# Spreading 1/den over each head's partitions: copies on the SP queue in place of 0/1 matrix products, in a one-core attention and gMLP kernel

## The chip, the cores and the metric

The kernel runs on one core of a Trainium2 chip. Its engines work side by side and meet through semaphores: TensorE (PE) multiplies matrices out of SBUF into PSUM, VectorE (DVE), ScalarE (ACT) and GpSimd (POOL) work on elements, SyncE (SP) issues DMA transfers. The metric is device time in microseconds (us) of one launch, lower is better.

## The reference

B = 1, S = 2048, D = 512, H = 32 heads of Dh = 16, F = 1792; inputs in bfloat16. The first block is linear attention, the second a gMLP that mixes along the sequence.

```python
def _A_ref(x, wqkv, wo):
    qkv = (x @ wqkv).reshape(B, S, 3, H, Dh).transpose(2, 0, 3, 1, 4)
    q, k, v = qkv[0], qkv[1], qkv[2]
    phi = lambda t: jnp.where(t > 0, t + 1, jnp.exp(t)) + 1e-06
    pq, pk = phi(q), phi(k)
    kv = jnp.einsum('bhsd,bhse->bhde', pk, v)
    z = jnp.einsum('bhsd->bhd', pk)
    num = jnp.einsum('bhqd,bhde->bhqe', pq, kv)
    den = jnp.einsum('bhqd,bhd->bhq', pq, z)[..., None] + 1e-06
    o = num / den
    return o.transpose(0, 2, 1, 3).reshape(B, S, D) @ wo

def _B_ref(x, w_in, w_sp, b_sp, w_out):
    z = gelu_tanh(x @ w_in)
    z1 = z[..., :Fh]
    z2 = _layernorm(z[..., Fh:])
    g = jnp.einsum('ts,bsf->btf', w_sp, z2) + b_sp[None, :, None]
    return (z1 * g) @ w_out

x = A_x
h = x + _A_ref(_layernorm(x), A_wqkv, A_wo)
h2 = h + _B_ref(_layernorm(h), B_w_in, B_w_sp, B_b_sp, B_w_out)
```

## The kernel before

The sequence is cut into 16 tiles of 128 rows; four tiles make a group of 512 (gq or tg, 0 to 3). The feature dimension of 512 lies in four chunks (c, 0 to 3) of 128 partitions, each with 8 heads of 16.

Stage by stage: tiles of x are loaded, normalised on DVE (L568 statistics, L572 aggregate, L603) and transposed into xT, tiles 0 to 5 on PE (L633), tiles 6 to 15 by DMA transposes on SP's queue (L625). PE makes K (L715) and Q (L729); phi is Exp and Relu on ACT (L692, L694) and one or two operations on DVE (L695, then L698 or L701). V is never made: PE sums x'K over all tiles (L747), and once that is complete makes K'V from it (L796). DVE masks K'V to its heads' diagonal blocks (L806), PE multiplies it by Wo (L814), and ACT and DVE copy the two halves out (L819, L821). With that, a group's attention output is phi(Q) times this matrix (L879), which DVE adds to x (L884).

Before L879, phi(Q) is divided by den. `den(gq)` multiplies phi(Q) by the summed keys (L829, four products into 32 partitions each, one row of 512 for each head), and ACT makes 1/den as Ln and Exp (L834, L836), in bfloat16 in `rb_v`. PE spreads each head's row over the head's 16 partitions with a 0/1 matrix `sel` (L844, four products with 32 rows, into PSUM). For chunks 0 and 1 ACT copies the result to SBUF (L854) and DVE multiplies from there (L856); for chunks 2 and 3 DVE multiplies straight out of PSUM (L859). POOL builds `sel` at the start (L542, L545).

The second block: h is normalised on ACT (L610), transposed by DMA on SP's queue into hT (L625), multiplied by w_in (L911 for z2, L942 for z1), with Gelu on ACT (L916, L947) and the layer norm of z2 on DVE. PE mixes z2 with w_sp' (L981); w_sp comes in through 64 DMA transposes on SP's queue (L957). The last product is w_out (L999), to which DVE adds h (L1005) and SP stores the tile (L1007); the last tile goes in two halves of 256 columns.

POOL issues the loads of Wv, w_in and Wo (L492), which wait for the landing of the last xT transpose; the first wsp transpose stands behind the same transpose on SP's queue.

Nothing decides at run time. Each `op` names its engine and what it reads and writes; `ORDER` is a list of all operations by number, written out by hand, from which each engine's own order follows, and `SLOT` gives the PSUM banks and buffers. Every engine works strictly in its order, and a wait stops whatever stands behind it on that engine. A DMA's issue is an operation of the engine that issues it. The numbers `cost` and `land` in an `op` don't change what runs.

Of the kernel before, what the change touches and what calls it, by code (L numbers as in the profile page):

```python
# [6 lines left out]
BF16 = mybir.dt.bfloat16  # L7
ACT = mybir.ActivationFunctionType
# [43 lines left out]
]  # L52
SLOT = [
# [301 lines left out]
def bass_sequential_preLN__linear_attn_block__mixer_gmlp__prompt_kernel(  # L355
# [29 lines left out]
    COPY_DVE = ()  # L385
    LN1 = [[0], [1], [2], [3], [4, 5], [6, 7], [8, 9], [10, 11], [12, 13], [14, 15]]
    N2_ACT = range(16)
    VIA_ACT = ((0, 0), (1, 0), (2, 0), (3, 0))
# [32 lines left out]
    gz2 = View(s_kv, 0, [NT, FH], BF16)  # L421
    mw = View(s_kv, NT * FH * 2, [KD, D], BF16)
# [16 lines left out]
    sel = small([P], BF16)  # L439
# [32 lines left out]
    def bank(i):  # L472
        return lambda a: a[:, i, :]
# [68 lines left out]
    op("pool", 0.2, lambda e: e.memset(sel.all().ap(), 0.0), w=[sel.all()], bias=BIG)  # L542
    sel3 = sel.ap.rearrange("p (b e) -> p b e", e=DH)
    for c in range(KD):
        op("pool", 0.35, lambda e, c=c: e.affine_select(  # L545
            sel3, sel3, pattern=[[-(CG * DH // P), P // DH], [0, DH]], compare_op=ALU.not_equal, fill=1.0,
            base=-CG * c, channel_multiplier=1), r=[sel.all()], w=[sel.all()], bias=BIG)

# [274 lines left out]
    def den(gq):  # L823
        t = Tile(PS)
        r_ = pqT[gq].all()

        def mm(e):
            for c in range(KD):
                i = e.matmul(t(bank(0)).ap()[CG * c:CG * (c + 1), :], lhsT=zb.ap[:, CG * c:CG * (c + 1)],  # L829
                             rhs=r_.ap()[:, c, :], start=True, stop=True)  # L830
            return i
        op("pe", 0.23, mm, r=[zb.all(), r_], w=[t()], land=3.0)
        rr, rb = rr_v[gq, :], rb_v[gq, :]
        op("act", act_c(512, 1), lambda e: e.activation(rr.ap(), t(bank(0)).ap(), ACT.Ln, bias=eps[1:2].ap(),  # L834
                                                        scale=1.0), r=[t(), eps[1:2]], w=[rr])
        o = op("act", act_c(512), lambda e: e.activation(rb.ap(), rr.ap(), ACT.Exp, scale=-1.0), r=[rr],  # L836
               w=[rb])
        last_lnexp.append(o)
        spread = {0: Tile(PS, 2), 2: Tile(PS, 2)}

        def sp_(e):
            for c in range(KD):
                q0 = CG * c
                k = e.matmul(spread[c // 2 * 2](bank(c % 2)).ap(), lhsT=sel.ap[q0:q0 + CG, :],  # L844
                             rhs=rb.ap()[q0:q0 + CG, :], start=True, stop=True)
            return k
        op("pe", 0.23, sp_, r=[sel.all(), rb], w=[spread[0](), spread[2]()], land=4.0)
        for c0 in (0, 2):
            t2 = spread[c0]
            d = pqT[gq][c0:c0 + 2, :]  # L850
            if (gq, c0) in VIA_ACT:
                e_ = Tile(EB)
                b_ = e_(lambda a: a[:, 0:2 * GW])
# [8 lines left out]
    for gq in range(NG):  # L862
        g.bias = -QGROUP * gq
        if gq:
            for f in (0, 2):
                q_proj(gq, f)
        den(gq)
# [210 lines left out]
```

## Time and profile before

| what | value |
|---|---|
| median of 3 runs | 244.15 us (244.04 to 244.27) |
| profiled execution's own time | 243.96 us |
| span of the profiled execution, first to last instruction | 242.2 us |
| granted TensorE clock | 1.00 |
| L844 on PE | 16 matmuls, 384 ns mean |
| L854 on ACT | 4, 1034 ns mean |
| L859 on DVE, out of PSUM | 4, 1204 ns mean |
| L856 on DVE, out of SBUF | 4, 681 ns mean |
| last two stores (64 KB each) | 1.5 us from issue to landing |

The span starts at the first instruction of the profiled execution; what is left of its own time, 1.8 us, lies before and after. Matmuls are pipelined, so the mean of one (379 ns for 512 columns) is longer than the distance between two starts; the timeline, which gives starts, tells how fast PE moves on. SP's time is time of issuing, not of the transfer.

### The profile page before, as it was taken

Reading aid. Unit: us, or ns where it says so; the run is one execution under the profiler, and the core shown is the slowest. Engines: PE = TensorE matmul, PEld = TensorE weight load, DVE = VectorE, ACT = ScalarE, POOL = GpSimd, SP = SyncE. Lnnn points to the kernel's source line nnn. Section 1 sums busy time; section 2 is a strip of 40 time slices with the busy share of each in tenths; the row PEclk is TensorE's granted clock in tenths of the full one; section 3 lists DMA queues with packets and bytes.
Section 4 is the critical chain, followed back from the end, with each engine's and each line's share of the span. In section 5 each row is a group of like instructions: output and inputs, shape, how many; then the busy total and the mean of one; then the engine's idle time right before and its main releaser. Section 6 shows DMA issues by size and latency. Waiting matters only on the chain.

```text
span 242.2 us, 3026 instructions
## 1 busy us (share of the span) xinstructions
PE 238.3 (98%) x1175; PEld 108.8 (45%) x1175; DVE 135.2 (56%) x269; ACT 85.1 (35%) x107; POOL 34.1 (14%) x87
## 2 busy tenths in 40 slices
PE   8999999999999999999999999999999999999995
PEld 3544443433444444445444444444444444444443
DVE  4999654589999967656533223251332513322443
ACT  3875744898588598564500010000000000000000
POOL 5316021002316542122100000000000000000000
DMA  6920459954324231459344444446200100000022
GB/s 199 321 43 18 94 106 337 232 122 96 46 43 128 47 46 22 87 119 231 88 108 92 107 86 95 100 108 94 83 0 0 65 24 0 0 0 3 0 87 87
DMA packets 55598, 21.57 MB, mean 89 GB/s; under 512 B 49472, under 2 KB 54720, under 8 KB 55584
## 3 DMA queue, kind: packets, MB, share of 16 engines
q1 hardware_dynamic: 54640, 17.05, 32.7%
q0 software_dynamic: 944, 4.33, 5.5%
q8 instruction: 9, 0.15, 0.3%
q14 instruction: 5, 0.04, 0.1%
HBM read 7.47 MB, written 2.10 MB: 40 GB/s over the span
## 4 chain that ended last, share of the span: by engine, by line
PE 91%; DVE 4%; DMA 2%; ACT 2%; SPq 1%; issue 0%
PE ps L981 40%; PE ps L942 10%; PE ps L911 10%; PE ps L999 10%; PE ps L747 6%; PE ps L879 5%; PE ps L715 5%; PE ps L729 4%; DMA xh<-in_A_x_dram 2%; DVE small L568 1%; SPq L492 1%; DVE xT_pq_z L698 1%; DVE xh L884 0%; DVE xT_pq_z L859 0%; DVE e L695 0%; PE ps L844 0%
## 5 line engine op out<-in xcount | busy, mean ns | idle before, releaser
L981 PE MATMUL ps<-wsp,pk_xn_z 128*128 128x512 bf16 x336 | 73.8, 379 | 0.0
L988 DVE TENSOR_TENSOR e<-ps,e 128x512 bf16<-128x512 f32 x28 | 19.4, 691 | 66.0 <-PE ps L981 66.0
L981 PEld LDWEIGHTS ps<-wsp,pk_xn_z 128*128 128x128 bf16 x336 | 32.8, 98 | 39.5
L942 PE MATMUL ps<-hT,win 128*128 128x512 bf16 x112 | 26.6, 379 | 0.0
L911 PE MATMUL ps<-win,hT 128*128 128x512 bf16 (+1 forms) x128 | 26.0, 353 | 0.0
L999 PE MATMUL ps<-wout,xT_pq_z 128*128 128x512 bf16 (+1 forms) x119 | 24.7, 367 | 0.0
L981 PE MATMUL ps<-wqkv_wsp,pk_xn_z 128*128 128x512 bf16 x112 | 24.3, 379 | 0.0
L947 ACT ACTIVATE xT_pq_z<-ps 128x1024 bf16<-128x1024 f32 (+1 forms) x16 | 14.4, 913 | 23.9 <-PE ps L942 23.9
L568 DVE BATCH_NORM_STATS2 small<-xh 128x6 f32<-128x512 bf16 x32 | 20.7, 678 | 3.3 <-DMA xh<-in_A_x_dram 3.3
L920 DVE BATCH_NORM_STATS2 small<-pk_xn_z 128x6 f32<-128x512 bf16 (+1 forms) x32 | 18.3, 611 | 7.2 <-ACT pk_xn_z L916 7.1
L692 ACT ACTIVATE e<-ps 128x1024 bf16<-128x1024 f32 x16 | 16.5, 1029 | 9.7 <-PE ps L715 6.1
L911 PEld LDWEIGHTS ps<-win,hT 128*128 128x128 bf16 x128 | 12.5, 98 | 12.7 <-ACT e L854 0.3
L916 ACT ACTIVATE pk_xn_z<-ps 128x896 bf16<-128x896 f32 x16 | 14.5, 914 | 8.9 <-PE ps L911 8.8
L1005 DVE TENSOR_TENSOR e<-ps,xh 128x512 bf16<-128x512 f32 (+1 forms) x17 | 11.2, 660 | 11.3 <-PE ps L999 11.3
L999 PEld LDWEIGHTS ps<-wout,xT_pq_z 128*128 128x128 bf16 x119 | 11.6, 98 | 12.8
L981 PEld LDWEIGHTS ps<-wqkv_wsp,pk_xn_z 128*128 128x128 bf16 x112 | 11.0, 98 | 13.2
L942 PEld LDWEIGHTS ps<-hT,win 128*128 128x128 bf16 x112 | 10.9, 98 | 12.6 <-ACT pk_xn_z L916 0.4
L589 POOL TENSOR_TENSOR small<-small 128x2 f32<-128x2 f32 x22 | 16.0, 727 | 1.2
L587 POOL TENSOR_SCALAR small<-small 128x2 f32<-128x2 f32 x22 | 6.4, 297 | 67.6 <-DVE small L572 67.4
L747 PE MATMUL ps<-pk_xn_z 128*128 128x512 bf16 x64 | 15.6, 379 | 0.0
L729 PE MATMUL ps<-xT_pq_z,wqkv_wsp 128*128 128x512 bf16 x64 | 15.5, 380 | 0.0
L715 PE MATMUL ps<-wqkv_wsp,xT_pq_z 128*128 128x512 bf16 x64 | 15.3, 379 | 0.0
(72 smaller groups left out, 191.0 us busy)
## 6 DMA issues: line engine op xcount, KB each, us to landing
out_dram<-e SPq DMA_DIRECT2D x15, 128.0 KB, 1.7
win<-in_B_w_in_dram POOLq DMA_DIRECT2D x1, 1792.0 KB, 9.2
xh<-in_A_x_dram SPq DMA_DIRECT2D x5, 256.0 KB, 4.7
wqkv_wsp<-in_A_wqkv_dram SPq DMA_DIRECT2D x2, 512.0 KB, 5.7
wout<-in_B_w_out_dram POOLq DMA_DIRECT2D x1, 896.0 KB, 6.4
wsp<-in_B_w_sp_dram SPq DMA_TRANSPOSE x48, 2.9
xh<-in_A_x_dram SPq DMA_DIRECT2D x1, 512.0 KB, 6.2
wqkv_wsp<-in_A_wqkv_dram POOLq DMA_DIRECT2D x1, 512.0 KB, 4.8
```

What stands on the lines that cost most here:

```text
L568: op("dve", dve_c(512), lambda e: e.bn_stats(s6.ap(), src.ap()), r=[src], w=[s6])
L589: return op("pool", 0.7, lambda e: e.tensor_tensor(dst.ap(), dst.ap(), h.ap(), ALU.pow), r=[dst, h], w=[dst])
L692: op("act", act_c(n), lambda e: e.activation(lo.ap(), t(flat).ap(), ACT.Exp), r=[t()], w=[lo])
L715: i = e.matmul(t(bank(ti)).ap(), lhsT=lhs.ap()[:, c, :], rhs=rhs.ap()[:, c, :], start=(c == 0), stop=(c == KD - 1))
L729: r_ = e.matmul(t(bank(i)).ap(), lhsT=lhs.ap()[:, c, :], rhs=rhs.ap()[:, c, :], start=(c == 0), stop=(c == KD - 1))
L747: r = e.matmul(txk[h](bank(i)).ap(), lhsT=xx.ap()[:, c * P:(c + 1) * P], rhs=kk.ap(), start=(n == 0), stop=(n == NT - 1))
L911: k = e.matmul(t(bank(i)).ap()[:, 0:b - a], lhsT=l.ap()[:, c, :], rhs=win[c, a:b].ap(), start=(c == 0), stop=(c == KD - 1))
L920: op("dve", dve_c(b - a), lambda e, s6=s6, src=src: e.bn_stats(s6.ap(), src.ap()), r=[src], w=[s6])
L942: k = e.matmul(t(bank(i)).ap(), lhsT=l.ap()[:, c, :], rhs=r_.ap()[:, c, :], start=(c == 0), stop=(c == KD - 1))
L981: k = e.matmul(t(bank(0)).ap(), lhsT=l.ap()[:, s - a, :], rhs=r_.ap()[:, s - a, :], start=(s == 0), stop=(s == NT - 1))
L988: op("dve", dve_c(512), lambda e: e.tensor_tensor(gb().ap(), t(bank(0)).ap(), bsp().ap()[:, tg * GW:(tg + 1) * GW], ALU.add), r=[t(), bsp( ...
L999: k = e.matmul(t(bank(0)).ap()[:, 0:b - a], lhsT=l.ap()[:, fc, :], rhs=wout[fc, a:b].ap(), start=(fc == 0), stop=(fc == KF - 1))
```

## The change

1/den no longer goes through PE. Each group and chunk gets one SBUF-to-SBUF DMA copy on SP's queue: its source is 8 rows of `rb` (every fourth partition of the chunk's 32, since a head's row stands in four equal copies), each read 16 times, its destination a buffer `r_v` of 128 partitions x 512. The buffers lie where phi(K) and the normalised x were (tiles 12 to 15 of phi(K) for group 0, the normalised x for groups 1 to 3), so a copy also waits for the L747 products that read these. Chunks 0 and 1, and chunks 2 and 3, share a semaphore each; DVE multiplies two chunks at a time, from SBUF. `sel`, its five POOL instructions, the ACT copies and the PSUM tiles for the spread are gone. The last tile's output is stored as 384 and 128 columns.

`ORDER` and `SLOT` are new throughout. Line numbers move: L844, L854 and L859 are gone, the product is L843, the copy L839, den L823, the mask of K'V L796 (was L806), the product with Wo L807 (was L814), its copy out L814 (was L821), the attention product L867 (was L879).

```diff
-    VIA_ACT = ((0, 0), (1, 0), (2, 0), (3, 0))
+    DEN = [(0,), (1,), (2,), (3,)]
...
+    r_v = [View(s_kv, (3 + i) * KD * GW * 2, [KD, GW], BF16) for i in range(NG)]
...
-    sel = small([P], BF16)
...
-    op("pool", 0.2, lambda e: e.memset(sel.all().ap(), 0.0), w=[sel.all()], bias=BIG)
-    sel3 = sel.ap.rearrange("p (b e) -> p b e", e=DH)
-    for c in range(KD):
-        op("pool", 0.35, lambda e, c=c: e.affine_select(
-            sel3, sel3, pattern=[[-(CG * DH // P), P // DH], [0, DH]], compare_op=ALU.not_equal, fill=1.0,
-            base=-CG * c, channel_multiplier=1), r=[sel.all()], w=[sel.all()], bias=BIG)
...
-        spread = {0: Tile(PS, 2), 2: Tile(PS, 2)}
-
-        def sp_(e):
-            for c in range(KD):
-                q0 = CG * c
-                k = e.matmul(spread[c // 2 * 2](bank(c % 2)).ap(), lhsT=sel.ap[q0:q0 + CG, :],
-                             rhs=rb.ap()[q0:q0 + CG, :], start=True, stop=True)
-            return k
-        op("pe", 0.23, sp_, r=[sel.all(), rb], w=[spread[0](), spread[2]()], land=4.0)
+
+    def spread_mul(gq):
+        rb = rb_v[gq, :]
+        for c in range(KD):
+            r = r_v[gq][c, :]
+            src = rb.ap()[CG * c:CG * (c + 1):CG * DH // P, :].unsqueeze(1).to_broadcast([P // DH, DH, GW])
+            op("sp", 0.5, lambda e, r=r, src=src: e.dma_start(r.ap(), src), r=[rb], w=[r],
+               dma=(f"r{gq}{c // 2}", True), nbytes=P * GW * 2)
         for c0 in (0, 2):
-            t2 = spread[c0]
-            d = pqT[gq][c0:c0 + 2, :]
-            if (gq, c0) in VIA_ACT:
...
-            op("dve", dve_c(1024), lambda e, t2=t2, d=d: e.tensor_tensor(flat(d.ap()), flat(d.ap()), t2(flat).ap(),
-                                                                         ALU.mult), r=[d, t2()], w=[d])
+            d, m = pqT[gq][c0:c0 + 2, :], r_v[gq][c0:c0 + 2, :]
+            op("dve", dve_c(1024, 2), lambda e, m=m, d=d: e.tensor_tensor(flat(d.ap()), flat(d.ap()), flat(m.ap()),
+                                                                          ALU.mult), r=[d, m], w=[d])
...
-        project(n, [(0, D)] if n < NT - 1 else [(0, D // 2), (D // 2, D)])
+        project(n, [(0, D)] if n < NT - 1 else [(0, D - P), (D - P, D)])
```

More of the change, by code (lines that the diff above doesn't have):

```diff
@@ L821, in bass_sequential_preLN__linear_attn_block__mixer_gmlp__prompt_kernel, with den @@
             op("dve", dve_c(1024), lambda e, t=t, d=d: e.tensor_copy(d.ap(), t().ap()), r=[t()], w=[d])
-    def den(gq):
-        t = Tile(PS)
-        r_ = pqT[gq].all()
+    def den(gs):
+        t = Tile(PS, len(gs))
+        r_ = [pqT[gq].all() for gq in gs]
         def mm(e):
-            for c in range(KD):
-                i = e.matmul(t(bank(0)).ap()[CG * c:CG * (c + 1), :], lhsT=zb.ap[:, CG * c:CG * (c + 1)],
-                             rhs=r_.ap()[:, c, :], start=True, stop=True)
-            return i
[L832 to L836, printed above, removed]
+            for j in range(len(gs)):
+                for c in range(KD):
+                    i = e.matmul(t(bank(j)).ap()[CG * c:CG * (c + 1), :], lhsT=zb.ap[:, CG * c:CG * (c + 1)],
+                                 rhs=r_[j].ap()[:, c, :], start=True, stop=True)
+            return i
+        op("pe", 0.23 * len(gs), mm, r=[zb.all()] + r_, w=[t()], land=3.0)
+        rr, rb = rr_v[gs[0]:gs[-1] + 1, :], rb_v[gs[0]:gs[-1] + 1, :]
+        op("act", act_c(512 * len(gs), 1), lambda e: e.activation(rr.ap(), t().ap(), ACT.Ln, bias=eps[1:2].ap(),
+                                                                  scale=1.0), r=[t(), eps[1:2]], w=[rr])
+        o = op("act", act_c(512 * len(gs)), lambda e: e.activation(rb.ap(), rr.ap(), ACT.Exp, scale=-1.0), r=[rr],
@@ L837, in den @@
                w=[rb])
         last_lnexp.append(o)
-        spread = {0: Tile(PS, 2), 2: Tile(PS, 2)}
-        def sp_(e):
-            for c in range(KD):
-                q0 = CG * c
-                k = e.matmul(spread[c // 2 * 2](bank(c % 2)).ap(), lhsT=sel.ap[q0:q0 + CG, :],
-                             rhs=rb.ap()[q0:q0 + CG, :], start=True, stop=True)
-            return k
-        op("pe", 0.23, sp_, r=[sel.all(), rb], w=[spread[0](), spread[2]()], land=4.0)
-        for c0 in (0, 2):
-            t2 = spread[c0]
-            d = pqT[gq][c0:c0 + 2, :]
-            if (gq, c0) in VIA_ACT:
-                e_ = Tile(EB)
-                b_ = e_(lambda a: a[:, 0:2 * GW])
-                op("act", act_c(1024), lambda e, t2=t2, b_=b_: e.activation(b_.ap(), t2(flat).ap(), ACT.Copy),
-                   r=[t2()], w=[b_])
-                op("dve", dve_c(1024, 2), lambda e, b_=b_, d=d: e.tensor_tensor(flat(d.ap()), flat(d.ap()), b_.ap(),
-                                                                               ALU.mult), r=[d, b_], w=[d])
-                continue
-            op("dve", dve_c(1024), lambda e, t2=t2, d=d: e.tensor_tensor(flat(d.ap()), flat(d.ap()), t2(flat).ap(),
-                                                                         ALU.mult), r=[d, t2()], w=[d])
@@ new lines, in spread_mul @@
+    def spread_mul(gq):
+        rb = rb_v[gq, :]
+        for c in range(KD):
+            r = r_v[gq][c, :]
+            src = rb.ap()[CG * c:CG * (c + 1):CG * DH // P, :].unsqueeze(1).to_broadcast([P // DH, DH, GW])
+            op("sp", 0.5, lambda e, r=r, src=src: e.dma_start(r.ap(), src), r=[rb], w=[r],
+               dma=(f"r{gq}{c // 2}", True), nbytes=P * GW * 2)
+        for c0 in (0, 2):
+            d, m = pqT[gq][c0:c0 + 2, :], r_v[gq][c0:c0 + 2, :]
+            op("dve", dve_c(1024, 2), lambda e, m=m, d=d: e.tensor_tensor(flat(d.ap()), flat(d.ap()), flat(m.ap()),
+                                                                          ALU.mult), r=[d, m], w=[d])
@@ L866, in bass_sequential_preLN__linear_attn_block__mixer_gmlp__prompt_kernel @@
                 q_proj(gq, f)
-        den(gq)
+        for gs in DEN:
+            if gs[-1] == gq:
+                den(gs)
+                for j in gs:
+                    spread_mul(j)
     for gq in range(NG):
```

84 rows, old and new, of tables (ORDER, SLOT) are left out of this document.

## The prediction

> **What bounds the kernel now.** I read the page first: the busy shares and the chain that ended last.
>
> ```profile
> PE 238.3 (98%) x1175; PEld 108.8 (45%) x1175; DVE 135.2 (56%) x269; ACT 85.1 (35%) x107; POOL 34.1 (14%) x87
> ...
> PE 91%; DVE 4%; DMA 2%; ACT 2%; SPq 1%; issue 0%
> ```
>
> TensorE (PE) is the bound: 98% busy, 91% of the chain. Next, the waits of PE, which name hardly one:
>
> ```profile
> PE ps L633 <- DVE pk_xn_z L603: 0.4, 1, 0.4
> ```
>
> So a matmul that goes shortens the run by its own time, and an idle microsecond of PE lengthens it by one. Third, PE's timeline where the change sits (start, length of the merged row, line):
>
> ```profile
> 44.37 0.61 PE L829 MATMUL ps<-xT_pq_z,small 128*32 128x512 bf16 x8
> 44.91 1.04 PE L729 MATMUL ps<-xT_pq_z,wqkv_wsp 128*128 128x512 bf16 x4
> 45.79 1.06 PE L796 MATMUL ps<-wsp,wqkv_wsp 128*128 128x128 bf16 x16
> 46.78 0.40 PE L844 MATMUL ps<-wsp,small 32*128 32x512 bf16 x4
> 47.10 1.04 PE L729 MATMUL ps<-xT_pq_z,wqkv_wsp 128*128 128x512 bf16 x4
> 47.98 1.03 PE L814 MATMUL ps<-wqkv_wsp,wsp 128*128 128x512 bf16 x4
> ```
>
> Read the starts: 4 full matmuls move PE on by 0.86 (0.216 each), L796's 16 by 1.0, four spreads (L844) by 0.32. Last, the queue that the new copies must share, SP's own timeline (issues; the length is SP's time):
>
> ```profile
> 14.38 18.60 SPq L625 DMA_TRANSPOSE xT_pq_z<-pk_xn_z  x10
> 33.02 25.87 SPq L957 DMA_TRANSPOSE wsp<-in_B_w_sp_dram  x16
> 38.45 4.66 SPq L957 DMA_TRANSPOSE wsp<-in_B_w_sp_dram  x1
> 51.11 2.56 SPq L957 DMA_TRANSPOSE wsp<-in_B_w_sp_dram  x2
> 103.44 26.72 SPq L957 DMA_TRANSPOSE wsp<-in_B_w_sp_dram  x20
> ```
>
> A transpose normally takes SP 1.31 (26.72 / 20, one hold of 0.7 included). The first wsp transposes take longer: the fifth holds SP for 4.66, and the eleventh starts at 51.11, 18.1 after the first; ten at 1.31 would be 13.1. That is 5.0 of hold. The windows view says why: from 34 to 47 us all 16 DMA engines are 0.96 busy, with the three weight loads (2.8 MB) that POOL issues on the same event that starts the wsp transposes, the landing of the last xT transpose.
>
> **What is removed.** Four groups of L844 at 0.33 = 1.3. Ahead of three of them PE lost about 0.1 more (eight L729 before 50.66 take 1.82, not 1.73), and before the one at 56.99 about 0.3, waiting for Exp. All of it is on the path: -1.9. The four ACT copies (L854, 1.03 each) and the DVE products out of PSUM (1.2, now 0.68 from SBUF) are off the path, as are five POOL instructions at the start: nothing. The last store: PE does the same 512 columns; the DVE add of 128 columns takes 0.29 (row of L780's shape) for 0.42, but it stands behind the longer add of 384, and its issue behind a 0.33 issue: 0 +- 0.1.
>
> **What is moved.** In the changed kernel's built order, den(0) and den(1) stand 22 L747 matmuls earlier on PE, and on DVE the normalisations of tiles 8 to 15 come earlier. The DVE work ahead of tile 12's (16 statistics at 0.60, 15 aggregates at 0.10, 14 normalisations at 0.31, phi 5 x 0.33 + 2 x 0.60 + 1.12) is 19.4 from a start at 3.0; the same count for tile 8 in the old order gives 22.1 where its transpose issued at 22.62, so I add 0.5: tile 12 goes at 22.9, tile 15 three transposes later at 26.9 instead of 31.71. The wsp transposes and the weight loads, released together as before, then start 4.8 earlier, and so does their collision: the bytes are the same.
>
> **What is added.** On SP's queue: eleven wsp transposes, then r1 chunks 3 and 2, r0 chunks 0 and 1, r1 chunk 1, r0 chunks 2 and 3, a wsp, r1 chunk 0, four wsp, r2, four hT transposes, r3. SP gets to the first copy at 51.11 + 1.30 - 4.8 = 47.6; the eleventh transpose lands 2.9 after its issue, at 49.2. Issuing a copy costs SP 0.5 (four stores from 168.37 take 2.04).
>
> How long a copy moves is not in the trace; the nearest rows, each with 128 KB, in the windows view (DMA share is the last but one number):
>
> ```profile
> 28.00:30.60 2.60, 2.60 (x14) 1.19 (x13) 1.07 (x3) 2.44 (x3) 0.00 (x0) 1.00 0.49 99
> 190.00:191.00 1.00, 1.00 (x7) 0.41 (x6) 0.69 (x1) 0.00 (x0) 0.00 (x0) 1.00 0.39 131
> ```
>
> A store fills the engines for 0.39 (whole inside 190 to 191), an SBUF-to-SBUF transpose for 0.49 x 1.31 = 0.64. I take 0.64: both of its ends are in SBUF, and a copy reads only 8 partitions 16 times over. The Trainium skill, DMA: Bandwidth & Descriptors, section on why a DMA increments its semaphore by 16 ("How many engines (k)"), has k as the largest number up to 16 that divides both sides' slowest dimension, here 8 and 128, so 8 engines. No run here shows it; it would make the store's 0.39 into 0.78: 248.4, a rival below.
>
> r0 chunks 0 and 1 are then in at 49.2 + 4 x 0.64 = 51.8 (store pace: 47.6 + 3 x 0.5 + 1.8 landing = 50.9), chunks 2 and 3 at 49.2 + 7 x 0.64 = 53.7 (52.4).
>
> Who waits for that: DVE, in order. Its new order is r1's product, r0's first product, the mask of K'V (L806), r0's second product, a phi pair (L695, L698), the copy of Wo's product (L821), so the mask and L821, which need no copy at all, are queued behind products that do.
>
> ```profile
> 46.88 0.69 DVE L806 TENSOR_TENSOR wsp<-ps,small 128x512 bf16<-128x512 f32 x1 [1.19 <-PE ps L796]
> ...
> 48.62 0.68 DVE L856 TENSOR_TENSOR xT_pq_z<-xT_pq_z,e 128x1024 bf16<-128x1024 bf16 x1
> ```
>
> Mask done at 51.8 + 0.68 + 0.69 and 0.1 of hand-over = 53.25, so L814 on PE starts at 53.3. PE is there at: L829 at 44.37 - 22 x 0.216 = 39.6, + 0.54, + 4.75 for the 22, + 1.73 (eight L729) + 1.0 (L796) + 1.75 (eight L729) = 49.35. **Idle 3.95** (store pace 3.05). L814 and eight L729 (2.6) bring PE to 55.9. DVE: r0's second product at 53.7 + 0.7 = 54.4, phi 0.43 + 0.60, L821 1.22: 56.65. The first L879 starts at 56.7: **idle 0.8** (0.35). For r2 the chain den, Ln 0.70, Exp 0.63, four copies (3.2 to 3.8), two products (1.3) is 6.0 to 6.6 against 32 matmuls, 6.9; DVE's queue may add some: 0 to 0.4, I take 0.2. Later work is pushed back as a whole; r3 and the 32 late wsp transposes have tens of microseconds.
>
> **Sum.** -1.9 + 3.95 + 0.8 + 0.2 = +3.05 on the profiled execution's 243.96 (span 242.2): 247.0. The runs' median, 244.15, is 0.19 above the profiled one, so 247.2.
>
> **Rivals.**
> Copies at the store's pace: -1.9 + 3.05 + 0.35 = +1.5, 245.7. For it: the store is the only plain DMA2D row out of SBUF.
> Copies at 0.78, half the engines: 52.3 and 54.7, so mask 53.8, idle 4.45; L821 57.65 against PE at 56.4, idle 1.3; with 0.4 for r2, +4.25: 248.4. For it: the source has 8 partitions, where every transfer of the trace has 128 on its SBUF side.
> The PE clock falls during the idle 4 us. The first matmuls show a slow pace: 12 of 512 columns take 5.25 from 0.83, weight loads 0.43 apart, until 5.07, so ten at 0.43 instead of 0.216 lose 2.1: 249.3. Against: PE is never idle for more than 0.4 after that, so the trace can't tell how long a pause it takes. The Trainium skill, TensorE: Matmul & The Clock Gate, "What's actually happening", puts the fall at an idle window of about 3.4 us that runs freely; a 4 us pause seldom holds a whole one.
> Faster: SP isn't held at the wsp transposes. At 1.31 each from 28.2, SP reaches the copies at 42.6, r0 is complete by 44.2 + 7 x 0.64 = 48.7, the mask goes when L796 ends, L821 ends at 51.6 before PE gets to L879 at 51.95, and only -1.9 + 0.2 is left: 242.5. For it: with wout's load in flight SP is held only 0.7 (from 103.44). Against: the same three loads follow the same event. It decides if SP gets to the first copy before about 43.6.
>
> **Chances.** Forecast (copies between 0.5 and 0.7) 0.32, half the engines 0.24, store pace 0.16, clock 0.14, not held 0.12, within 0.2% 0.02: faster 0.12, same 0.02, slower 0.86. About 0.2% (0.5 us) is what a measurement of this kernel can tell from no change. The range runs from 244.9 (store pace with 0.8 less of hold) to 249.5 (clock); it leaves out the faster case and a clock that falls on top of the slow copies.
>
> **What would show it.** PE's waits name L807 (the old L814) on DVE L796 with 3 to 4.5, then L867 on DVE L814 with 0.3 to 1.3; SP's timeline has the first copy near 47.6; DVE's waits name the copies' DMA at the product, L843. Wrong, if the copies start before 44, if PE's long wait stands elsewhere, or if matmuls after the wait are 0.43 apart.

## The result, and the profile after

| kernel | median us | runs | lowest to highest | profiled execution (span) | granted clock |
|---|---|---|---|---|---|
| before | 244.20 | 6 | 243.86 to 244.44 | 243.96 (242.2) | 1.00 |
| changed | 250.14 | 6 | 249.22 to 250.80 | 249.62 (247.9) | 0.993 in four runs, 0.986 in two |

The changed kernel takes 1.024 times as long (1.0211 to 1.027). Slower was expected, but only to 247.2, and 250.14 lies above the range's 249.5. Of the runs in the experiments below, one of experiment 1 (248.93) and one of experiment 4 (252.95, clock 0.986) are over 1.5% longer than the fastest of the same kernel and stand outside the ratios.

From the page of the changed kernel, the busy shares and the chain:

```profile
PE 236.6 (95%) x1137; PEld 108.5 (44%) x1159; DVE 132.5 (53%) x269; ACT 80.7 (33%) x103; POOL 32.0 (13%) x82
...
PE 88%; DMA 3%; DVE 3%; ACT 2%; SPq 1%; issue 1%; DVEq 0%; ACTq 0%
```

PE was 98% busy and is 95% busy: busy for 1.7 us less, in a span that is 5.7 us longer. It now waits. The waits of PE (us in total, times, longest):

```profile
PE ps L807 <- DVE wsp L799: 3.8, 1, 3.8
...
PE ps L930 <- ACT pk_xn_z L904: 0.6, 1, 0.6
PE ps L867 <- DVE xT_pq_z L843: 0.5, 1, 0.5
```

The mask of K'V is L799 in the profile (L796 in the text on record is the line above it). PE's timeline says where these waits stand (start, length of the merged row, line, idle before):

```profile
47.98 1.89 PE L722 MATMUL ps<-xT_pq_z,wqkv_wsp 128*128 128x512 bf16 x7
53.67 1.04 PE L807 MATMUL ps<-wqkv_wsp,wsp 128*128 128x512 bf16 x4 [3.81 <-DVE wsp L799]
54.54 3.18 PE L722 MATMUL ps<-xT_pq_z,wqkv_wsp 128*128 128x512 bf16 x8
57.52 2.33 PE L867 MATMUL ps<-pk_xn_z,xT_pq_z 128*128 128x512 bf16 x8
...
67.74 3.63 PE L867 MATMUL ps<-pk_xn_z,xT_pq_z 128*128 128x512 bf16 x16 [0.55 <-DVE xT_pq_z L843]
...
75.38 4.92 PE L930 MATMUL ps<-hT,win 128*128 128x512 bf16 x21 [0.55 <-ACT pk_xn_z L904]
```

Look at the second L722 row. Eight such matmuls take 1.89 elsewhere; here they take 3.18, and the next eight L867 2.33. The windows view of the same stretch has the reason in the third number from the right, the granted clock; the last two are DMA share and GB/s:

```profile
54.00:56.00 2.00, 2.00 (x9) 0.83 (x7) 1.41 (x3) 1.26 (x2) 0.00 (x0) 0.74 0.64 140
56.00:58.00 2.00, 2.00 (x7) 0.53 (x5) 2.00 (x4) 0.92 (x2) 0.00 (x0) 0.50 0.39 86
58.00:60.00 2.00, 2.00 (x12) 0.71 (x10) 1.19 (x4) 1.70 (x2) 0.00 (x0) 0.90 0.58 131
62.50:66.00 3.50, 3.45 (x17) 1.61 (x17) 3.48 (x9) 2.23 (x3) 1.51 (x4) 1.00 0.43 150
```

The trace's clock records put the half rate at 54.98 to 58.39, 3.41 us long. It begins 1.3 us after PE has resumed.

Upstream stands DVE, which works in order. Its timeline in the changed kernel:

```profile
50.87 0.69 DVE L843 TENSOR_TENSOR xT_pq_z<-xT_pq_z,pk_xn_z 128x1024 bf16<-128x1024 bf16 x1 [4.52 <-DMA pk_xn_z<-wsp]
52.32 0.69 DVE L843 TENSOR_TENSOR xT_pq_z<-xT_pq_z,pk_xn_z 128x1024 bf16<-128x1024 bf16 x1 [0.76 <-DMA pk_xn_z<-wsp]
52.93 0.68 DVE L799 TENSOR_TENSOR wsp<-ps,small 128x512 bf16<-128x512 f32 x1
54.56 0.69 DVE L843 TENSOR_TENSOR xT_pq_z<-xT_pq_z,pk_xn_z 128x1024 bf16<-128x1024 bf16 x1 [0.94 <-DMA pk_xn_z<-wsp]
```

Each product waits for two copies, and the first two products come 1.45 apart: 0.73 for a copy. The mask needs no copy and goes the moment the second product lets it. Behind that, SP's timeline:

```profile
28.30 19.06 SPq L945 DMA_TRANSPOSE wsp<-in_B_w_sp_dram  x11
47.41 4.81 SPq L839 DMA_DIRECT2D pk_xn_z<-wsp  x7
```

Eleven wsp transposes hold SP until 47.4, as forecast (47.6), while 1/den is ready at about 42 (experiment 1 issues the first copy then).

### The profile page after: what moved, and what is told of

Read it like the earlier page. It is cut to its first block, busy times and chain, and to the rows that moved or that the text cites. A ratio compares the mean times of both kernels' runs of the same rounds, so it can differ in the third digit from the quotient of the medians.

```text
span 247.9 us, 2975 instructions
## 1 busy us (share of the span) xinstructions
PE 236.6 (95%) x1137; PEld 108.5 (44%) x1159; DVE 132.5 (53%) x269; ACT 80.7 (33%) x103; POOL 32.0 (13%) x82
## 4 chain that ended last, share of the span: by engine, by line
PE 88%; DMA 3%; DVE 3%; ACT 2%; SPq 1%; issue 1%; DVEq 0%; ACTq 0%
PE ps L969 39%; PE ps L930 10%; PE ps L987 10%; PE ps L899 9%; PE ps L740 5%; PE ps L722 5%; PE ps L708 5%; PE ps L867 4%; DMA pk_xn_z<-wsp 2%; DMA xh<-in_A_x_dram 1%; DVE xT_pq_z L843 1%; SPq L839 1%; PE ps L626 1%; ACT wsp L828 1%; DVE small L561 1%
## 5 line engine op out<-in xcount | busy, mean ns | idle before, releaser
L930 PE MATMUL ps<-hT,win 128*128 128x512 bf16 x109 | 26.0, 379 | 0.7 <-ACT pk_xn_z L904 0.6
L987 PE MATMUL ps<-wout,xT_pq_z 128*128 128x512 bf16 (+2 forms) x118 | 24.6, 366 | 0.1
L993 DVE TENSOR_TENSOR e<-ps,xh 128x512 bf16<-128x512 f32 (+2 forms) x17 | 11.1, 660 | 11.4 <-PE ps L987 11.4
L930 PEld LDWEIGHTS ps<-hT,win 128*128 128x128 bf16 x112 | 10.9, 98 | 13.6 <-ACT pk_xn_z L904 0.9
L582 POOL TENSOR_TENSOR small<-small 128x2 f32<-128x2 f32 x22 | 16.5, 752 | 1.3
L722 PE MATMUL ps<-xT_pq_z,wqkv_wsp 128*128 128x512 bf16 x62 | 16.0, 404 | 0.1
L867 PE MATMUL ps<-pk_xn_z,xT_pq_z 128*128 128x512 bf16 x62 | 15.0, 387 | 0.7 <-DVE xT_pq_z L843 0.5
L904 ACT ACTIVATE pk_xn_z<-ps 128x896 bf16<-128x896 f32 x16 | 14.0, 919 | 4.8 <-PE ps L899 4.7
L580 POOL TENSOR_SCALAR small<-small 128x2 f32<-128x2 f32 x22 | 5.8, 263 | 74.8 <-DVE small L565 74.5
L740 PE MATMUL ps<-pk_xn_z 128*128 128x512 bf16 x62 | 14.5, 379 | 0.6 <-DVE pk_xn_z L694 0.4
```

The costliest lines, as they stand in the source:

```text
L582: return op("pool", 0.7, lambda e: e.tensor_tensor(dst.ap(), dst.ap(), h.ap(), ALU.pow), r=[dst, h], w=[dst])
L722: r_ = e.matmul(t(bank(i)).ap(), lhsT=lhs.ap()[:, c, :], rhs=rhs.ap()[:, c, :], start=(c == 0), stop=(c == KD - 1))
L740: r = e.matmul(txk[h](bank(i)).ap(), lhsT=xx.ap()[:, c * P:(c + 1) * P], rhs=kk.ap(), start=(n == 0), stop=(n == NT - 1))
L867: i = e.matmul(t(bank(ti)).ap(), lhsT=l.ap()[:, c, :], rhs=mw[c, :].ap(), start=(c == 0), stop=(c == KD - 1))
L930: k = e.matmul(t(bank(i)).ap(), lhsT=l.ap()[:, c, :], rhs=r_.ap()[:, c, :], start=(c == 0), stop=(c == KD - 1))
L987: k = e.matmul(t(bank(0)).ap()[:, 0:b - a], lhsT=l.ap()[:, fc, :], rhs=wout[fc, a:b].ap(), start=(fc == 0), stop=(fc == KF - 1))
```

## The experiments

The theory after the result: the copies are late because SP reaches them late; they are slow because they run on half of the engines; DVE's order hands that lateness to the mask, which needs none of it; and the pause costs PE its clock. The rivals: the copies are slow enough to cost the time wherever they stand, or the half clock is what delays everything. Ratios are to runs of the kernel before on the same chip.

**1. SP's order alone.** Copies of r0 and r1 ahead of the transposes that get held.

```diff
 # SP's queue in order (ORDER); c = chunk
-wsp x11, r1 c3, r1 c2, r0 c0, r0 c1, r1 c1, r0 c2, r0 c3, wsp, r1 c0, wsp x4, r2 x4, hT x4, r3 x4
+wsp x4, r1 c3, r1 c2, r0 c0, r0 c1, r1 c1, r0 c2, r0 c3, r1 c0, wsp x6, r2 x4, wsp, hT x4, r3 x4
```

> The changed kernel with twelve of the sixteen first wsp transposes moved behind the copies on SP's queue (six behind the copies of r0 and r1, one behind r2, one behind r3, two each into later gaps); nothing else. Theory (the copies come late because they stand behind transposes that the weight loads hold): SP issues the first copy near 42 instead of 47.4, PE's waits at L807 (3.8) and L867 fall below 0.3, the granted clock stays 1.000; 4.9 off for the waits and 0.5 to 1.9 for the clock, so 244.2, from 243.6 to 245.0. Rival (the copies themselves are too slow, wherever they stand): L807 still waits over 2.5, 249 to 250.

Measured: 244.04, ratio 0.9999 (0.9984 to 1.0014), clock 1.00. SP's timeline of this kernel:

```profile
28.47 5.24 SPq L945 DMA_TRANSPOSE wsp<-in_B_w_sp_dram  x4
42.01 5.46 SPq L839 DMA_DIRECT2D pk_xn_z<-wsp  x8
```

The first copy goes at 42.0 instead of 47.4; L807 starts without a wait, the first L867 starts 0.24 after the matmuls ahead of it would let it, and the clock holds. The whole of the loss is gone with one queue's order, the copies as slow as before. What is not there is a gain: waits of 0.54 for r2's product and 0.55 at L930 remain.

**2. The copy's source alone.** All 32 rows of the chunk are read, each 4 times, so that 16 engines share a copy.

```diff
-src = rb.ap()[CG * c:CG * (c + 1):CG * DH // P, :].unsqueeze(1).to_broadcast([P // DH, DH, GW])
+src = rb.ap()[CG * c:CG * (c + 1), :].unsqueeze(1).to_broadcast([CG, P // CG, GW])
```

> The changed kernel with each copy reading all 32 rows of its chunk 4 times, not every fourth row 16 times; same bytes, same values. Theory (8 source partitions put a copy on 8 of the 16 DMA engines): 32 rows use 16, a copy's share in the windows view over its own time doubles, r0's first two chunks land 0.6 earlier, L807 waits 3.2 to 3.4; 249.5 if the clock still falls, 248.3 if that shorter wait spares it. Rival (the repeats, not the partitions, set the pace): landing, waits and time as now, 250.1 within 0.4.

Measured: 249.24, ratio 1.02 (1.0175 to 1.0225), clock 0.993 in all four runs. Its first line of PE's waits:

```profile
PE ps L807 <- DVE wsp L799: 3.2, 1, 3.2
```

Each copy now lands 2.5 to 2.8 after its issue, in step with SP's issues, which are 0.65 apart. So SP's issuing becomes the limit, the wait shrinks by 0.6 only, and a 3.2 us pause costs the clock too. The slow copy is a second cause, not the first; how much it costs in this place is not settled, since the interval overlaps that of the changed kernel (1.0211 to 1.027).

**3. The pause filled.** 16 matmuls of ones, whose result is overwritten, ahead of L807.

```diff
+fill = op("pe", 16 * MM, lambda e: [e.matmul(fill_t(bank(0)).ap(), lhsT=ones_row[:, 0:P], rhs=ones_row,
+                                             start=True, stop=True) for _ in range(16)][-1])
```

> The changed kernel with 16 matmuls of ones (128 x 512) on PE ahead of L807, into the bank that L807 then writes; they add work and no wait. Theory (PE's pause makes the clock fall): L807 waits under 0.6, granted clock 1.000 in every run; the first L867 still waits for DVE's copy of Wo's product, now visibly, about 1.2, so only what the slow clock lost behind it comes back: 249.2, and the runs lie within 0.4 of each other. Rival (the clock falls for another reason): 0.986 to 0.993 again and 250.1. If the pause doesn't cost as I think, over 251.

Measured: 249.01, ratio 1.0204 (1.0178 to 1.023), clock 1.00 in every run; the runs lie 1.35 apart, where 0.4 was expected. PE's waits between 45 and 60 us:

```profile
PE ps L867 <- DVE pk_xn_z L814: 1.1, 1, 1.1
PE ps L807 <- DVE wsp L799: 0.6, 1, 0.6
```

The clock falls because of the pause, and not because of the copies' traffic, which is the same here. And at full speed PE waits 1.1 at L867, for the product copied out behind r0's late chunks: in the changed kernel half speed fills that wait. The clock's net price is the difference of the ratios, 1.024 - 1.0204 = 0.0036, some 0.9 us, but the two intervals overlap, and two of the changed kernel's runs had the clock down for twice as long (0.986). Between the two profiled executions it is less: from the start of L807 to den of group 2 (L823, at 59.78 and at 59.26) PE takes 6.11 in the changed kernel and 5.67 here, so 0.44 for one stretch of half clock.

**4. DVE's order alone.** The mask and L814 ahead of the three products that wait.

```diff
 # DVE's order
-r1 c2-3, r0 c0-1, mask L799, r0 c2-3, phi pair, L814, r1 c0-1
+mask L799, phi pair, L814, r1 c2-3, r0 c0-1, r0 c2-3, r1 c0-1
```

> The changed kernel with the mask L796, the phi pair and the copy L814 moved on DVE ahead of the products of r1 and r0 that wait for copies; the copies stay where they are. Theory (the mask is late only because it is queued behind these products): L807 waits under 0.3, and the wait goes to the first L867, 2.7 to 3.2, for r0's second product, with 0.8 at den(2) behind it; 1.4 off, 248.5, or 247.5 if the shorter pause spares the clock. Rival (L807 waits for something else): 3.8 stays, 250.1.

Measured: 247.63, ratio 1.013 (1.0106 to 1.0155). PE's waits between 45 and 60 us:

```profile
PE ps L867 <- DVE xT_pq_z L843: 2.6, 1, 2.6
```

L807 starts at 49.62 without a wait; the wait moves to L867, which does need r0's products, and is 2.6 long (2.7 to 3.2 expected). It has become shorter by what PE could do meanwhile, and is then set by the copies alone. The 0.8 expected at den of group 2 doesn't show: PE runs at half speed from 56.14 on and gets there only at 57.53. The clock fell in two of the three runs that the ratio rests on, and stayed at 1.00 in the shortest, 247.13.

**5 and 6. Both orders and the source put right, with either last store.** In SP's order of experiment 1, with the source of experiment 2:

```diff
 # SP:  r2's copies
-one of c0-1, both of c2-3, the other of c0-1
+one of c0-1, one of c2-3, the other of c0-1, the other of c2-3
 # DVE: around r2 and r3
-phi product L691 (r3's first half), statistics, r2 c0-1, r2 c2-3
+statistics, r2 c0-1, r2 c2-3, phi product L691; three later operations also change places
 # PE:  start of the second block
-z2 of tiles 0 and 1 (L899), then six groups of z1 (L930)
+z2 of tile 0 and of tile 1's first half, one group of z1, tile 1's second half, then z1
 # last tile's store, experiment 5 only
-project(n, [(0, D)] if n < NT - 1 else [(0, D - P), (D - P, D)])
+project(n, [(0, D)] if n < NT - 1 else [(0, D // 2), (D // 2, D)])
```

> The copies of r0 and r1 ahead of the held wsp transposes (as in the first experiment), sources of 32 rows, r2's copies with chunks 0 and 1 first, DVE's two r2 products ahead of one phi(Q) multiplication (L691) and r3's phi ahead of some statistics, the first two z1 products (L930) ahead of the table load's wait, and the last store again 256 and 256. Theory: what ate the 1.9 us of the removed products in the first experiment (244.04) is three things, and each is gone here: the wait for r2's product (0.54), the wait for the Gelu behind the table load (0.55), and the tail (0.18). 244.0 - 0.54 - 0.55 - 0.18 = 242.8, PE without a wait over 0.3 after 12 us. Rival: the table load and r2's chain only hand the wait on to the next instruction of PE; then 243.6 to 244.0, with waits at L899 or L867.

> The kernel of e5 with the last store 384 and 128 columns, as in the change. Theory: the split costs 0.15 to 0.2 (from PE's last matmul to the end of the span 2.65 instead of 2.47), so 0.17 above e5, about 242.95. Rival, the prediction's 0 +- 0.1: the same as e5 within 0.05.

Measured: experiment 5 242.99 (242.48 to 243.59), ratio 0.9949 (0.9931 to 0.9967); experiment 6 243.06 (242.42 to 245.31), ratio 0.9954 (0.9931 to 0.9976). PE's waits of experiment 5 from 12 us to the end are these, and nothing else:

```profile
PE ps L823 <- DVE xT_pq_z L691: 0.2, 1, 0.2
PE ps L740 <- issue: 0.2, 1, 0.2
```

So the kernel without the products, put into an order in which nothing new waits, is 1.2 us faster than the one before; the order and the products were not taken apart. Of the two stores, the profiles say 0.2 for 384/128: from PE's last matmul to the end of the span 242.2 - 239.73 = 2.5 before and 240.9 - 238.40 = 2.5 in experiment 5, but 247.9 - 245.25 = 2.65 in the changed kernel and 241.9 - 239.20 = 2.7 in experiment 6. The medians, 0.07 apart, can't confirm so little.

**7. The load of w_in later.** SP's order is the changed kernel's.

```diff
+g.ops[208].deps[g.ops[241]] = True      # the load of w_in also waits for r0's last copy
 # POOL's order
-Wo, w_in, Wv
+Wo, Wv, w_in
```

> The changed kernel with one edit: the load of w_in (1.8 of the 2.8 MB that POOL issues) also waits for the landing of r0's last copy. Nothing in SP's order is changed. Theory: SP is held at the wsp transposes by the weight loads; with 1.0 MB left beside them the hold is at most 1.8, the first copy is issued at 42.6 to 44.4, L807 waits 0 to 1.0, the clock stays up, 244.0 to 245.2. Rival: the transposes hold SP by themselves (their number, or their ring), the first copy stays at 47, L807 waits 3.8: 249.6.

Measured: 246.82, ratio 1.0113 (1.0085 to 1.0141), clock 1.00. From SP's timeline, and from DVE's:

```profile
28.26 14.86 SPq L945 DMA_TRANSPOSE wsp<-in_B_w_sp_dram  x11
43.17 4.79 SPq L839 DMA_DIRECT2D pk_xn_z<-wsp  x7
```

```profile
63.14 1.29 DVE L843 TENSOR_TENSOR xT_pq_z<-xT_pq_z,pk_xn_z 128x1024 bf16<-128x1024 bf16 x2 [1.55 <-DMA pk_xn_z<-wsp]
```

The mechanism is as expected: eleven transposes take 14.9 instead of 19.1, the first copy goes at 43.2, L807 doesn't wait. The time is a miss by 1.6 of the expectation's upper end. Two waits of PE were not in it: 1.15 at the first L867, since at 0.73 each r0's last copies are late even from 43.2 on; and 1.68 at r2, since w_in now moves from 50.7 to 58.4, with the DMA engines 0.97 busy from 51 to 58, beside the wsp transposes queued ahead of r2's copies. The collision was not removed, it was handed to r2.

**8. Half of the fill.**

```diff
-fill = op("pe", 16 * MM, ... for _ in range(16)][-1])
+fill = op("pe", 8 * MM, ... for _ in range(8)][-1])
```

> The changed kernel with 8 matmuls of ones (128x512, into the bank that L807 writes next) ahead of L807, where e3 had 16: the wait starts at 51.4 instead of 49.7 and is 2.2 long instead of 3.8 (e3: 0.6). Theory: the clock falls by how much of a 3.4 us window is idle, so with 2.2 idle (0.65 of a window) it stays up in most runs: mean clock 1.000, 249.0. Rival: any pause of 2 us or more does it: clock 0.993 or less in every run, 249.3 to 250.2.

Measured: 248.78, ratio 1.0186 (1.016 to 1.0212). PE waits 1.79 at L807, less than the 2.2 expected; the clock was 1.00 in three runs and 0.993 in one. By the length of the pause:

| kernel | PE's longest pause near 50 us (profiled execution) | runs with a fallen clock |
|---|---|---|
| changed | 3.81 | 6 of 6 |
| 2, source of 32 rows | 3.22 | 4 of 4 |
| 4, DVE's order | 2.63 | 2 of 3 |
| 8, half filled | 1.79 | 1 of 4 |
| 3, filled; 7, w_in late | 1.1 (3), 1.15 and, at r2, 1.68 (7) | none in the profiles; the mean is 0.999 or 1.00 in all runs |

A rule by which every pause over 2 us costs the clock isn't borne out (experiment 4 escapes once), nor one by which shorter pauses never do (experiment 8 is caught once). What decides is how a pause falls on a grid. In each profiled execution of the changed kernel and of the experiments, the changes of the clock lie whole multiples of 3.413 us apart (in the changed kernel 3.78, then 54.98, which is 15 such stretches later, then 58.39); the first one comes at 3.78 to 6.76, so the grid lies differently from execution to execution. The pause of the changed kernel falls on two stretches, that of experiment 8 on one (windows view; the second number is the length, the third PE's busy time):

```profile
48.15:51.57 3.42, 1.66 (x7) 0.59 (x6) 0.69 (x1) 2.10 (x3) 0.00 (x0) 1.00 0.46 157
51.57:54.98 3.41, 1.31 (x7) 0.60 (x8) 1.72 (x3) 0.24 (x1) 0.00 (x0) 1.00 0.62 165
```

```profile
50.62:54.03 3.41, 1.62 (x9) 0.54 (x7) 1.86 (x3) 0.24 (x1) 0.00 (x0) 1.00 0.70 185
```

The stretches with 1.66 and 1.62 of busy time, 51% and 52% idle, kept the clock. The one with 1.31, 62% idle, lost it at its end, and so did one of experiment 4 (idle for 2.26, 66%) and one of experiment 2 (busy for 0.35, 90% idle). In these executions the limit lies between 52% and 62% of a stretch. A pause of about 2 us reaches that only if the grid doesn't cut it, so that the same kernel can lose the clock in one run and keep it in the next, as those of experiments 4 and 8 do.

## Why the prediction was wrong

**Right.** The direction, the place and the mechanism. SP reached the first copy at 47.41 (47.6 forecast), tile 15's transpose went at 26.99 (26.9), the hold was in place, and experiment 7 shows that the weight loads make it. L807 stood for 3.97 between its expected start without a wait, 49.70, and 53.67; the forecast was 3.95. That hit is partly luck: the mask was 0.35 later than forecast and so was PE's arrival. The removed products' -1.9 is borne out in most: PE ends at 238.40 in experiment 5 and at 239.73 before, 1.33 earlier; with the 0.17 that it still waits and 0.1 by which it reaches den later (39.74 against 44.37 - 22 x 0.216 = 39.62), 1.6 of the 1.9 is found.

**Wrong, step by step**, in the order of the sum:

- *"I take 0.64" for a copy.* It took 0.73, the rival with half the engines (0.78). r0's chunks landed at 52.30 and 54.53, that rival's 52.3 and 54.7, not at 51.8 and 53.7. The fourth row of the windows fence shows it: r2's four copies keep the 16 engines 0.43 x 3.50 = 1.5 busy, 0.38 each, the store's pace, yet copies land 0.73 apart; so half of the engines carry them. The trace's packet records say the same: each of these copies ends with 8 packets of 4 bytes, and with 16 in experiment 2. The Trainium skill, DMA: Bandwidth & Descriptors, "How many engines (k)", gave this number of engines, and the trace agrees. The step that failed was to weigh the 0.64 of a transpose, whose two sides have 128 partitions, above the one feature that set this copy apart.
- *"Issuing a copy costs SP 0.5"*, from the stores. It cost 0.61, one every 0.65 (0.82 for the first).
- *"Idle 0.8" at the first L867.* Without the slow clock it is 1.1 (experiment 3), the rival's 1.3.
- *"I take 0.2" for r2.* It was 0.55. DVE's first product of r2 (chunks 0 and 1) needs the last of the four copies, and starts 4.76 after the first copy's issue at 61.60, where 3.2 to 3.8 was taken for the copies; DVE is idle ahead of it, so the wait is the copies' and not DVE's queue:

```profile
66.36 1.32 DVE L843 TENSOR_TENSOR xT_pq_z<-xT_pq_z,pk_xn_z 128x1024 bf16<-128x1024 bf16 x2 [0.38 <-DMA pk_xn_z<-wsp]
```

- *Not in the sum: L930.* 0.55 for the first Gelu, which stands behind r3's Ln and Exp and a table load:

```profile
72.46 0.63 ACT L830 ACTIVATE wsp<-wsp 128x512 bf16<-128x512 f32 x1
73.11 1.28 ACT L904 ACT_TABLE_LOAD   x1
```

  Before, the same load stood there (67.36) and PE had other work to hand; the new order brings L930 to wait on it. Experiment 5 has no such wait, with one group of z1 products moved ahead on PE.
- *"0 +- 0.1" for the last store.* 0.2 in the profiles. I had seen that the second issue stands behind the first, and didn't price it.
- *"The PE clock falls", 0.14.* It fell in every run. The argument against it, that a 4 us pause seldom holds a whole window, was a step that failed too: in the profiled execution the 3.41 us ahead of the half rate (51.57 to 54.98) were idle for 2.10 only, 62%, and in experiment 4 (52.74 to 56.15) for 2.26, 66%. That these stretches are the ones that decide follows from the grid under experiment 8: each is one whole stretch of it. The Trainium skill, TensorE: Matmul & The Clock Gate, "What's actually happening", has the fall after at least one idle window of about 3.4 us; the length agrees, but the window need not be idle throughout. The price of 2.1 was too high in turn: the half rate lasted 3.41, and most of what it costs fills the 1.1 that PE would have waited at L867. 0.44 is left between the profiled executions, 0.9 between the medians.

Put together, with what was measured in place of each term: -1.6 for the products, 3.97 at L807, 1.1 at the first L867, 0.55 for r2, 0.55 for L930 and 0.2 for the store are +4.8, so 249.0 from 244.2; experiment 3, the changed kernel with its clock kept, has 1.0204 x 244.2 = 249.2. The fallen clock makes up the rest to 250.1; that rest is a difference of two medians and no check of its own. The half-engine rival's 248.4 comes near in part by luck: it has 0.5 too much at L807, and nothing for L930 and the store. Against the forecast's 247.2, 2.9 were missing: 0.9 for the clock, which had no term in the sum, 0.55 for L930, 0.35 more for r2, 0.3 more at the first L867, 0.3 less gained by the products and 0.2 for the store make 2.6, and 0.3 is not accounted for. The range left out exactly this: "a clock that falls on top of the slow copies". I had treated the two as alternatives, though nothing ties them: the slow copies lengthen the very pause that costs the clock.

One difference between the two profiled executions can't be put down to the change: the wait of PE for an early tile (L626, the old L633) was 0.4 before and 1.1 after, and 0.4 to 1.0 in the kernels of the experiments, which don't differ from the changed kernel there.

Open: why the clock was down for two stretches (0.986) in two of the six runs. A pause of 3.81 cut in the middle would leave two stretches 56% idle each, between the 52% that kept the clock and the 62% that lost it; no profile of such a run was taken.

## What to carry to other kernels

Work that leaves a bound engine for a DMA queue is paid for where that queue is at that moment: before pricing the transfer, read when the queue gets to it, what lies in flight beside it, and which instructions that need nothing of it stand behind its consumer. Moving the issue ahead of the held transfers recovered all of the 2.4%; making the transfer faster in its old place recovered 0.4%, and that with overlapping intervals. Costs that share a cause are added, not listed as alternatives, and a pause of 2 us or more on TensorE gets a price for the clock as well as for the time.

## What the runs showed of the hardware that was not expected

- A pause of 3.2 us or more halved the TensorE clock in 10 of 10 runs, one of 2.6 in 2 of 3, one of 1.8 in 1 of 4. The half rate came late, 0.35 to 1.3 us after work had resumed in the three profiled executions that show it, and lasted 3.41 us. The clock changed only on a grid of 3.413 us; a stretch of it that was idle for 62% or more lost the clock, one of 52% kept it.
- A copy from 8 partitions to 128 took 0.73, nearly twice the 0.39 of a 128-partition store of as many bytes: the same work (0.38 of all 16 engines), on half of the engines. Reading 32 rows instead let each land 2.5 to 2.8 after its issue, but an issue of this shape costs SP 0.61, so that the queue's issuing became the limit.
- A later load moved the collision: w_in in flight from 50.7 to 58.4 delayed r2's copies, which it had not touched before, by more than a microsecond.
